# Copies of a finished AFNO chunk: from one DMA queue after the slot's other work to two queues right behind the second layer

## The chip, the core and the metric

The kernel runs on one core of one Trainium2 chip. A core has five instruction streams that run side by side and wait for each other by semaphores: TensorE (PE, matmuls; its weight loads are shown apart as PEld), VectorE (DVE), ScalarE (ACT), GpSimd (POOL) and SyncE (SP, which here only issues DMAs). Sixteen DMA engines carry out what the streams issue. The metric is the device time of one execution in microseconds (us), smaller is better; the figure for a kernel is the median of several runs.

## The reference

The whole layer works on `x` of 4096 rows (a sequence of 4096 points) by 640 features, in float32:

```python
h = _layernorm(x, axis=-1) * (1 + ca) + sa
x = x + ga * _A_ref(h, A_w1, A_b1, A_w2, A_b2)   # AFNO: rfft, a two-layer complex MLP per frequency, soft shrink, irfft
h = _layernorm(x, axis=-1) * (1 + cb) + sb
x = x + gb * _B_ref(h, B_w_gate, B_w_up, B_w_down)   # SwiGLU: (silu(h@wg) * (h@wu)) @ wd, 640 -> 1728 -> 640
```

The six vectors `sa, ca, ga, sb, cb, gb` come from `silu(c) @ w_mod`. The AFNO part takes the Fourier transform along the 4096 points, then for each frequency and each of 4 blocks of 160 features a first complex layer with ReLU and a second complex layer, then a shrink by 0.01, and transforms back.

## The kernel before

The program has three parts in time: a first stage (load, layer norm, first step of the Fourier transform), the AFNO part, and the SwiGLU part, whose order is written out by a planner with costs and due times. The change lies in the AFNO part alone, whose order is written out by hand: each engine runs its instructions in the order in which the Python program issues them, and semaphores are put in for every dependence.

The frequencies are cut into 8 chunks (`ch`), and each chunk into 4 blocks of features (`b`). The loop over `p = 4*ch + b` goes through 29 slots, and the last three slots are written out behind it. One slot works on several (chunk, block) pairs at different depths of the pipeline; `on(f, k)` calls `f(k // 4, k % 4)`:

- `stage_l1(p)`, L679 to L697: first complex layer, on PE, with ReLU and splitting into a high and a low float32 half on ACT and DVE.
- `stage_b` and `evac_b` (L618 to L626) and `evac_rh`, `evac_rl` (L648, L658): second Fourier step of a later chunk and its copies out of PSUM.
- `stage_l2(p - 1)`, L729 and L731: second complex layer on PE. DVE adds the bias and writes the result into the tiles `tt`: two tiles per chunk, `tts[ch, 0]` and `tts[ch, 1]`, each of 128 frequencies by real and imaginary part by 640 features. The pool has two buffers for `tt`, so a chunk's two tiles lie in the buffers that the chunk before it used. Block `b` fills its 160 columns; a tile is complete after `stage_l2` of block 3, which runs in the first slot of the next chunk. In the slot after that, `stage_l2` of the next chunk's block 0 writes into the same buffers.
- `move_x(ch - 1, i)`, L741 to L746, for i = 0 to 3: the copies that this case is about. For each i, two DMAs of 64 partitions by 640 floats bring the real and the imaginary half of 64 frequencies from `tt` into the two halves of a tile `xx` of 128 partitions. i = 0, 1 read `tts[ch, 0]`; i = 2, 3 read `tts[ch, 1]`. `xx` has 5 buffers. In each first slot of a chunk (`b == 0`) from the second chunk on, so 7 times, 8 such DMAs are issued.
- `shrink_parts(p - 5)` on ACT (L751, L752), `shrink(p - 6)` on DVE (L757, or L759 and L760 near the end), `shrink_high(p - 6)` on ACT (L766), `shrink_low(p - 6)` on DVE (L771): the shrink of one `xx` tile and its splitting into `xh` and `xl`. `shrink_low` is the last reader of `xx`.
- `stage_i(p - 7)`, L782 to L786: first inverse Fourier step on PE, copy to `co` on ACT (L785; two buffers), and a store of `co` to the scratch tensor `s2` in device memory, issued by POOL (L786).
- On SP, besides the moves: the slot's loads of `w_mod` rows (tile `wm`, L553; one buffer; DVE sums them up in `acc`, L558 and L560), in every fourth slot the next chunk's input `g` and table `tb` (L313, L299), and near the end parts of `s2` (L843).

On POOL the AFNO slots hold only the `s2` stores (L786) and, around the chunk that carries the edge frequencies (`ch == CE`), some small copies (L629 to L662, L803, L804).

Of the kernel before, what the change touches and what calls it, by code (L numbers as in the profile page):

```python
# [173 lines left out]
def body(tc, x, w1, b1, w2, b2, wg, wu, wd, c, wm, k_fa, k_tb, k_tx, k_bm, k_bx, k_ga, k_ge, k_id, out, dbg=None):  # L174
    nc = tc.nc
    pe, act, dve, pool = nc.tensor, nc.scalar, nc.vector, nc.gpsimd
# [25 lines left out]
    with ExitStack() as top:  # L202
# [35 lines left out]
        with ExitStack() as af:  # L238
# [40 lines left out]
            def weights_high(w, h, l, v, sg, eng=None):  # L279
                if eng:  # L280
                    eng.tensor_scalar(w[:, :, h], v, sg, None, op0=OP.mult)
                else:
                    act.activation(w[:, :, h], v, AF.Copy if isinstance(sg, float) else AF.Identity, scale=sg)

            def weights_low(w, h, l, v, sg):
                dve.scalar_tensor_tensor(w[:, :, l], v, sg, f32(w[:, :, h]), op0=OP.mult, op1=OP.subtract)
# [10 lines left out]
            def load_tb(ch):  # L297
                tb = lp.tile([P, 4, 128], F32, tag="tb", bufs=2, name=f"tb{ch}")
                nc.sync.dma_start(tb, k_tb[:, 4 * ch:4 * ch + 4])  # L299
                tbs[ch] = tb  # L300


            def load_g(ch, us=None):
                if ch not in gs:
                    gs[ch] = fx.tile([P, 4, D], F32, tag="gx", bufs=2, name=f"g{ch}")
                if ch < 2:
                    src = s1[0].rearrange("(u v) (q j e) d -> e u (v q) j d", u=4, e=2, q=4)[ch]
                    for u in us:
                        nc.sync.dma_start(gs[ch][u:P:4], src[u])
                else:  # L310
                    f, e = (1, 2) if ch < 4 else (2, 4)
                    src = s1[f].rearrange("(u v) (q e j) d -> e u (v q) (j d)", u=4, e=e, q=4)[ch % e]
                    nc.sync.dma_start(gs[ch].rearrange("p j d -> p (j d)"), src.rearrange("u r d -> r u d"))  # L313
# [230 lines left out]
            w, h, l, v, _ = prep2[5]  # L544
# [62 lines left out]
            tts = {}  # L607
# [4 lines left out]
            def stage_b(ch, t, tag=None):  # L612
                g, tb = gs[ch], tbs[ch]
                pb = (ps.tile([P, 2, 256], F32, tag=tag, name=f"pb{ch}_{t}") if tag else
                      bank0(1 if t == 4 else 0, [P, 2, 256], f"pb{ch}_{t}"))
                col = slice(128 * t, 128 * t + 128)
                for j in range(4):
                    mm(pb[:, :, 64 * j:64 * j + 64], g[:, j, col], tb[:, j, :], start=True, stop=True)  # L618
                pbs[ch, t] = pb

            def evac_b(ch, t):
                pb = pbs[ch, t]
                z = lp.tile([P, 2, 2, 258], F32R, tag="z", bufs=4, name=f"z{ch}_{t}")
                zs[ch, t] = z
                act.activation(z[:, 0, :, 0:256], pb, AF.Identity, scale=ca1[:, t:t + 1])
                dve.scalar_tensor_tensor(z[:, 1, :, 0:256], pb, ca1[:, t:t + 1],  # L626
                                         f32(z[:, 0, :, 0:256]), op0=OP.mult, op1=OP.subtract)
                if ch == CE:
                    pool.tensor_copy(z[:, 0, :, 0:257:256], f32(edge[:, 0, t]))  # L629
                    pool.tensor_copy(z[:, 1, :, 0:257:256], f32(edge[:, 1, t]))  # L630
                    pool.tensor_copy(z[:, :, :, 257], zero[:, 0, 0])
# [106 lines left out]

            xxs = {}

            def move_x(ch, i):  # L741
                q, h = i // 2, i % 2
                xx = p2.tile([P, D], F32, tag="xx", bufs=5, name=f"xx{ch}_{i}")
                for r in range(2):
                    nc.sync.dma_start(xx[64 * r:64 * r + 64, :], tts[ch, q][64 * h:64 * h + 64, r, :])
                xxs[ch, i] = xx  # L746


# [92 lines left out]
            def load_first_rows(lo, hi, q, e=slice(0, D)):  # L841
                for k in range(2):
                    q.dma_start(cf[k][lo:hi, :, e], s2[lo:hi, 2 * k:2 * k + 2, e])  # L843
# [4 lines left out]
            for p in range(LAST + 1):  # L848
                ch, b = p // 4, p % 4
                on(shrink, p - 6)  # L850
                on(stage_l1, p)


                if p < 4:
                    todo = ([(0, 2)], [(0, 3)], [(1, 4), (1, 0)], [(1, 1)])[p]
                elif b == 0:
                    todo = [(ch, 3)]
                else:
                    todo = [(ch + 1, 4)] * (b == 1) + [(ch + 1, b - 1)]
                todo = [q for q in todo if q[0] < NCH]  # L860
                for q in todo:
                    stage_b(*q)
                    if q[1] < 4:
                        evac_b(*q)
                for f, *a in sums.get(p, ()):
                    f(*a)

                rows = [p + 2] * (p < 4) + [p + 3] * (p > 2)
                for k in rows:
                    on(evac_rh, k)  # L870
                on(tail_l1, p)
                on(shrink_high, p - 6)
                for k in rows:
                    on(evac_rl, k)
                on(tail_low, p)
                on(stage_l2, p - 1)
                if p == 3:
                    stage_b(1, 2)
                    evac_b(1, 2)
                on(stage_i, p - 7)  # L880
                on(shrink_low, p - 6)
                if p < LAST:
                    on(shrink_parts, p - 5)
                if b == 0 and ch:
                    for i in range(4):
                        move_x(ch - 1, i)
                if p == 0:
                    for n in (3, 4):
                        weights_high(*prep2[n])
                    for job in prep2[2:5]:  # L890
                        weights_low(*job)
                if p == 0:
                    pool.dma_start(bm.rearrange("p a b c -> p (a b c)"), k_bm)
                if p == 2 or b == 3 and 2 < ch + 2 < NCH:
                    load_g(ch + 2)
                    load_tb(ch + 2)
                for f, *a in mods.get(p, ()):
                    f(*a)
                if p == LAST - 4:
                    cf += [rp.tile([P, 2, D], F32, tag=tag, name=f"cf{tag}") for tag in ("rm", "rr")]  # L900
                    load_first_rows(rb + 16, rl, nc.sync)
                elif p == LAST - 1:
                    load_first_rows(0, rb - 16, nc.sync)
# [153 lines left out]
        with ExitStack() as ff:  # L1057
# [1081 lines left out]
            for t in range(NS):  # L2139
                for n in range(NW):  # L2140
                    if sum_at(n) == t:
                        a, b = sum_w(n)
# [69 lines left out]
```

## Time and profile before

| what | value |
|---|---|
| median of 3 runs (lowest, highest) | 1471.63 us (1467.69, 1474.02) |
| the profiled execution's own time | 1472.98 us |
| its span, from the first to the last instruction | 1471.2 us |
| mean granted TensorE clock | 0.991 |
| AFNO slots that hold moves | from 94.2 to 277 us of the span |
| PE busy | 1432.1 us (97%) |
| DVE busy | 1054.7 us (72%) |
| ACT busy | 781.7 us (53%) |
| POOL busy | 413.4 us (28%) |

The profile is one execution. A line such as `L731 DVE` is line 731 of the kernel on VectorE; `tt<-pc,b2t` names the tile written and the tiles read. The bracket at the end of a line of the timeline tells how long the engine stood idle before it and what ended that. `SPq` and `POOLq` are DMA issues by SP and POOL. In a view by windows of time, each engine has its busy time and, in brackets, the number of instructions; then come the granted clock, the busy share of the DMA engines and what they moved in GB/s.

### The profile page before, as it was taken

To read this page: it belongs to the slowest core of one execution; us is meant where nothing else is said; L and a number is where in the kernel's file an instruction comes from. 1 tells how busy PE (TensorE), PEld (TensorE's weight loads), DVE (VectorE), ACT (ScalarE), POOL (GpSimd) and SP (SyncE) were. 2 spreads that over 40 slices of the span, in tenths; PEclk is the share of its full clock that TensorE was granted. 3 is DMA by queue.
4 is the path that set the end of the run, shared out by engine and by line. 5 is a ranking of instruction groups with operands and counts; after the bars stand their busy time and mean duration, and the time that the engine had idled before them with its cause. 6 is when DMAs were issued, how large, how long until landed. Compare 5 with 4: busy or idle time off the path is not lost.

```text
span 1471.2 us, 23664 instructions
## 1 busy us (share of the span) xinstructions
PE 1432.1 (97%) x8656; PEld 1353.6 (92%) x8656; DVE 1054.7 (72%) x1901; ACT 781.7 (53%) x1517; POOL 413.4 (28%) x529
## 2 busy tenths in 40 slices
PE   8899999989999999999999999999999999999999
PEld 4699999858878888899999999999999999999998
DVE  8968888877787787657777767787656566466653
ACT  7779989744445455435554545545453344344331
POOL 4500200055544344312433322433411121111111
PEclk9999999989999999999999999999999999999999
DMA  9956566656777986796775995776884345944422
GB/s 361 326 198 205 162 184 210 204 177 224 235 263 241 337 280 206 263 370 197 235 245 191 334 353 181 248 231 215 324 290 137 120 149 195 355 135 144 143 76 83
DMA packets 155927, 332.06 MB, mean 226 GB/s; under 512 B 19873, under 2 KB 79073, under 8 KB 154018
## 3 DMA queue, kind: packets, MB, share of 16 engines
q1 hardware_dynamic: 147426, 313.99, 63.1%
q0 software_dynamic: 6800, 13.93, 2.9%
q10 hardware_dynamic: 1584, 2.62, 0.5%
q8 instruction: 68, 1.11, 0.3%
q14 instruction: 49, 0.40, 0.1%
HBM read 234.35 MB, written 86.64 MB: 218 GB/s over the span
## 4 chain that ended last, share of the span: by engine, by line
PE 69%; issue 9%; DVE 9%; DMA 8%; ACT 3%; POOL 2%; SPq 1%; POOLq 0%; DVEq 0%; ACTq 0%
PE pd L2085 23%; PE pw L1890 8%; PE pw L1892 7%; PE pw L1891 7%; PE pg L1813 3%; PE pg L1814 3%; PE pg L1815 3%; PE pw L1901 2%; PE pw L1903 2%; PE pw L1902 2%; DMA cr<-s 2%; DVE st_a L193 2%; PE py L1533 1%; DMA wt<-td 1%; DVE wb L1347 1%
## 5 line engine op out<-in xcount | busy, mean ns | idle before, releaser
L2085 PE MATMUL pd<-wdh,a 128*128 128x320 f32 x1672 | 381.3, 310 | 1.5 <-DVE x L2057 1.1
L2085 PEld LDWEIGHTS pd<-wdh,a 128*128 128x128 f32 x1672 | 283.0, 188 | 2.5 <-DVE x L2057 1.4
L2085 PE MATMUL pd<-wdl,a 128*128 128x320 f32 x868 | 267.3, 309 | 0.0
L2057 DVE TENSOR_TENSOR x<-x,pd 128x320 f32<-128x320 f32 x384 | 178.2, 481 | 93.9 <-PE pd L2085 90.7
L1347 DVE TENSOR_TENSOR wb<-r,wb 128x512 fp32r<-128x512 f32 (+3 forms) x170 | 167.8, 994 | 16.1 <-ACT wb L1340 15.0
L2085 PEld LDWEIGHTS pd<-wdl,a 128*128 128x128 f32 x868 | 163.1, 188 | 0.5
L1890 PE MATMUL pw<-h,wt 128*128 128x384 f32 x416 | 141.6, 340 | 5.0 <-DMA wt<-td 2.9
L1444 ACT ACTIVATE wdh<-wdr 128x640 fp32r<-128x640 f32 x84 | 60.9, 733 | 149.8 <-PE pd L2085 142.2
L1892 PE MATMUL pw<-h,wt 128*128 128x384 f32 x416 | 140.2, 337 | 0.0
L1891 PE MATMUL pw<-h,wt 128*128 128x384 f32 x416 | 140.0, 337 | 0.0
L1340 ACT ACTIVATE wb<-r 128x768 fp32r<-128x768 f32 (+3 forms) x168 | 115.3, 701 | 20.3 <-PE pg L1815 11.7
L1934 POOL TENSOR_TENSOR sg<-s_x,sg 128x384 f32<-128x384 f32 x24 | 26.4, 1101 | 339.1 <-DVE s_x L1916 304.6
L1890 PE MATMUL pw<-h,wb 128*128 128x384 f32 x312 | 105.0, 337 | 0.0
L1892 PE MATMUL pw<-h,wb 128*128 128x384 f32 x312 | 104.6, 335 | 0.0
L1891 PE MATMUL pw<-h,wb 128*128 128x384 f32 x312 | 104.6, 335 | 0.0
L1937 DVE TENSOR_TENSOR a<-sg,a 128x384 fp32r<-128x384 f32 x104 | 80.2, 775 | 32.9 <-ACT a L1936 32.6
L1813 PE MATMUL pg<-ht,wb 128*128 128x512 f32 x260 | 103.7, 399 | 0.0
L1814 PE MATMUL pg<-ht,wb 128*128 128x512 f32 x260 | 102.0, 392 | 0.0
L1815 PE MATMUL pg<-ht,wb 128*128 128x512 f32 x260 | 101.6, 391 | 0.0
L1448 DVE TENSOR_TENSOR wdl<-wdr,wdh 128x640 fp32r<-128x640 f32 x84 | 74.6, 898 | 27.2 <-ACT wdh L1444 27.1
L1890 PEld LDWEIGHTS pw<-h,wt 128*128 128x128 f32 x416 | 78.6, 189 | 7.8 <-DMA wt<-td 3.5
L1516 POOL TENSOR_TENSOR cr<-cr,gab 128x640 f32<-128x640 f32 x28 | 48.2, 1720 | 119.3 <-DMA cr<-s 116.4
(278 smaller groups left out, 3380.7 us busy)
## 6 DMA issues: line engine op xcount, KB each, us to landing
wt<-td SPq DMA_DIRECT2D x104, 512.0 KB, 5.2
hs<-ho SPq DMA_DIRECT2D x52, 512.0 KB, 5.1
h<-hs SPq DMA_DIRECT2D x32, 768.0 KB, 9.9
r<-in_B_w_up_dram SPq DMA_DIRECT2D x36, 640.0 KB, 5.7
r<-in_B_w_gate_dram SPq DMA_DIRECT2D x36, 640.0 KB, 5.1
wdr<-wdd SPq DMA_DIRECT2D x35, 640.0 KB, 4.1
td<-wt SPq DMA_DIRECT2D x25, 512.0 KB, 4.7
xx<-tt SPq DMA_DIRECT2D x56, 160.0 KB, 3.8
```

Source lines behind the costliest of these rows:

```text
L1340: def high(ks, e=slice(0, c), copy=lambda o, i: act.activation(o, i, AF.Copy)):
L1347: dve.tensor_tensor(wbs[t, n][:, 1, ks, e], raw[t, n][:, ks, e], f32(wbs[t, n][:, 0, ks, e]), op=OP.subtract)
L1448: dve.tensor_tensor(l[:, f], wdraw[t, p][:, f], f32(h[:, f]), op=OP.subtract)
L1813: mm(b, wh, hh, start=(kk == 0), stop=False)
L1814: mm(b, wh, hl, start=False, stop=False)
L1815: mm(b, wl, hh, start=False, stop=(kk == 4))
L1890: mm(b, w(0, kp), a[:, kp, 0], start=start and kp == 0, stop=False, skip_group_check=not start)
L1891: mm(b, w(0, kp), a[:, kp, 1], start=False, stop=False, skip_group_check=not start)
L1892: mm(b, w(1, kp), a[:, kp, 0], start=False, stop=kp == 1, skip_group_check=not start)
L1937: Step("V", cv_ + 0.1, lambda: dve.tensor_tensor(o[:, 1], sg, f32(o[:, 0]), op=OP.subtract), (("ah", key),), ("act", t, fc, a), free=("sg" ...
L2057: dve.tensor_tensor(x2[:, e], x2[:, e], x[0][:, :320], op=OP.add)
L2085: mm(pd[g, hf][0][:, :320], l, m, start=i == 0, stop=i == len(s) - 1 and not (last and len(gs) > 1))
```

## The change

`move_x` gets a parameter for the engine that issues its DMAs. Its calls are put forward within the slot: they stand right behind `stage_l2(p - 1)` now, ahead of `stage_i(p - 7)`, `shrink_low(p - 6)` and `shrink_parts(p - 5)`. The copies for i = 0 and 1 stay on SP, and those for i = 2 and 3 are issued by POOL.

```diff
-            def move_x(ch, i):
+            def move_x(ch, i, eng=nc.sync):
                 q, h = i // 2, i % 2
                 xx = p2.tile([P, D], F32, tag="xx", bufs=5, name=f"xx{ch}_{i}")
                 for r in range(2):
-                    nc.sync.dma_start(xx[64 * r:64 * r + 64, :], tts[ch, q][64 * h:64 * h + 64, r, :])
+                    eng.dma_start(xx[64 * r:64 * r + 64, :], tts[ch, q][64 * h:64 * h + 64, r, :])
                 xxs[ch, i] = xx
...
                 on(stage_l2, p - 1)
+                if b == 0 and ch:
+                    for i in range(4):
+                        move_x(ch - 1, i, pool if i > 1 else nc.sync)
                 if p == 3:
...
                 if p < LAST:
                     on(shrink_parts, p - 5)
-                if b == 0 and ch:
-                    for i in range(4):
-                        move_x(ch - 1, i)
                 if p == 0:
```

In the order that results, the instructions of PE, ACT and DVE are the same and in the same order as before. On SP, 28 of the 56 moves are gone and nothing else changes place. On POOL, four moves stand in each of the seven slots ahead of that slot's store of `co`; in the slot p = 12 they stand behind the two small edge copies L803 and L804. From the second of the seven slots on, the tile `xx` of i = 3 lies in the buffer that `shrink_low(p - 6)` of the same slot still reads, so its copies wait for that instruction of DVE, before the change and after it.

## The prediction

> **What bounds the kernel now.** The page's first table says which engine is full over the whole span.
>
> ```profile
> PE 1432.1 (97%) x8656; PEld 1353.6 (92%) x8656; DVE 1054.7 (72%) x1901; ACT 781.7 (53%) x1517; POOL 413.4 (28%) x529
> ```
>
> PE is, but the change touches only the AFNO slots, some 200 us of 1471, so I read these by themselves: the windows view in stretches of about one chunk, with one row for all that follows.
>
> ```profile
> 100.00:128.00 28.00, 26.99 (x207) 26.38 (x206) 24.35 (x48) 25.31 (x53) 1.13 (x2) 1.00 0.54 167
> 128.00:158.00 30.00, 28.76 (x226) 28.50 (x226) 25.19 (x51) 26.90 (x56) 3.50 (x12) 1.00 0.58 182
> 158.00:188.00 30.00, 29.66 (x227) 28.97 (x226) 25.59 (x50) 28.02 (x59) 6.74 (x27) 1.00 0.58 176
> 188.00:220.00 32.00, 30.04 (x240) 29.45 (x239) 26.30 (x52) 27.95 (x57) 2.17 (x4) 1.00 0.56 174
> 220.00:248.00 28.00, 28.00 (x221) 28.00 (x220) 24.42 (x48) 27.12 (x56) 2.17 (x4) 1.00 0.54 175
> 248.00:279.00 31.00, 29.53 (x223) 28.82 (x222) 26.25 (x52) 25.22 (x54) 2.71 (x5) 1.00 0.67 210
> 300.00:1471.20 1171.20, 1152.24 (x6765) 1103.17 (x6763) 801.79 (x1363) 536.89 (x1023) 355.83 (x412) 0.99 0.67 225
> ```
>
> After the length come PE, PEld, DVE, ACT and POOL. PE stands still for only 1.01, 1.24, 0.34, 1.96, 0.00 and 1.47 us in the six chunks, and ACT and DVE are close behind it. So whatever the change frees elsewhere, **a chunk can hardly shrink by more than its idle time on PE**. The last row says that behind 300 us PE is busy 1152 of 1171 us: what AFNO saves shifts that part forward as a block, and I count it in full.
>
> Next, the view of waits, from 80 to 300 us, for DVE, ACT and PE.
>
> ```profile
> DVE tt L731 <- DMA xx<-tt: 12.0, 6, 2.7
> ACT r L704 <- DVE u L697: 7.9, 8, 1.9
> PE pi L782 <- DVE u L697: 1.9, 2, 1.2
> PE pl L679 <- DVE tt L737: 1.8, 1, 1.8
> PE pc L729 <- DVE tt L731: 0.4, 1, 0.4
> ```
>
> The first row is DVE's largest wait: the add that fills `tt` for a new chunk waits until the moves have read the old chunk out of that buffer. The timeline shows this, first slot and second slot of a chunk (the first two lines are the first boundary, then the second one with SP and POOL, then the waits of the other five).
>
> ```profile
> 93.69 0.89 DVE L731 TENSOR_TENSOR tt<-pc,b2t 128x320 f32<-128x320 f32 x2
> ...
> 100.14 0.49 DVE L731 TENSOR_TENSOR tt<-pc,b2t 128x320 f32<-128x320 f32 x1
> 103.36 0.49 DVE L731 TENSOR_TENSOR tt<-pc,b2t 128x320 f32<-128x320 f32 x1 [2.73 <-DMA xx<-tt]
> ...
> 121.29 0.89 DVE L731 TENSOR_TENSOR tt<-pc,b2t 128x320 f32<-128x320 f32 x2
> 121.81 6.26 SPq L745 DMA_DIRECT2D xx<-tt  x8
> 121.93 0.54 POOL L786 DMA_DIRECT2D s<-co  x1 [6.41 <-ACT co L785]
> 122.09 0.81 DVE L771 TENSOR_TENSOR xl<-xx,xh 128x640 fp32r<-128x640 f32 x1
> 128.11 0.49 DVE L731 TENSOR_TENSOR tt<-pc,b2t 128x320 f32<-128x320 f32 x1
> 128.16 5.12 SPq L553 DMA_DIRECT2D wm<-in_w_mod_dram  x2
> 130.66 0.49 DVE L731 TENSOR_TENSOR tt<-pc,b2t 128x320 f32<-128x320 f32 x1 [2.06 <-DMA xx<-tt]
> 160.87 0.49 DVE L731 TENSOR_TENSOR tt<-pc,b2t 128x320 f32<-128x320 f32 x1 [1.88 <-DMA xx<-tt]
> 190.52 0.49 DVE L731 TENSOR_TENSOR tt<-pc,b2t 128x320 f32<-128x320 f32 x1 [2.35 <-DMA xx<-tt]
> 222.21 0.49 DVE L731 TENSOR_TENSOR tt<-pc,b2t 128x320 f32<-128x320 f32 x1 [1.64 <-PE pl L679]
> 250.75 0.49 DVE L731 TENSOR_TENSOR tt<-pc,b2t 128x320 f32<-128x320 f32 x1 [1.74 <-DMA xx<-tt]
> 280.67 0.49 DVE L731 TENSOR_TENSOR tt<-pc,b2t 128x320 f32<-128x320 f32 x1 [1.23 <-DMA xx<-tt]
> ```
>
> SP starts the moves as soon as the first `tt` is full (121.81, against 121.29 + 0.49), so no instruction ahead of them in the program holds them back. They take SP 6.26 us for eight, and the last lands too late. The first add of the next chunk (128.11) does not wait; the second, which needs the moves of i = 2 and 3, waits 2.06 us. At the fifth boundary the view names PE, but I take the 1.64 us for the same wait, since it stands at the same place of a chunk. Seven waits: 13.6 us.
>
> **The change part by part.** *The place.* Putting the calls forward in the slot moves them past instructions of PE, DVE and ACT, which SP and POOL do not run. On SP nothing is passed. On POOL the moves now stand ahead of the slot's `s2` store. Alone the place is worth 0, by the 121.81 above; what it buys is that POOL does not wait for `co` first.
>
> *The split.* What one issue costs on either stream comes from the views of lines 745, 786 and 318 (the last are small copies of the first stage, on POOL and SP).
>
> ```profile
> L745 SPq DMA_DIRECT2D xx<-tt x56: 469/590/1893, 94.2 to 276.3; - x56
> DMA to landing us min/median/max: 2.6/3.8/5.7
> ...
> L786 POOL DMA_DIRECT2D s<-co x28: 542/542/591, 114.9 to 298.8; - x28
> DMA to landing us min/median/max: 2.4/3.9/6.3
> ...
> L318 POOL DMA_DIRECT2D g<-xa x4: 572/597/797, 45.2 to 49.8; - x4
> DMA to landing us min/median/max: 2.5/3.7/4.8
> ```
>
> POOL has never issued these moves, so its price lies between the nearest rows: 0.54 us (L786) and 0.80 us (the longest of L318). I take 0.6, the median of L318, whose copies go from SBUF to SBUF as the moves do. Four issues put the last one's start 3 x 0.6 = 1.8 us behind the end of the pair of adds, and it lands 3.9 us later: 5.7 us. With the ends of the rows it is 3 x 0.54 + 2.4 = 4.0 to 3 x 0.8 + 6.3 = 8.7 us. At the first boundary the pair ends at 94.58 and the second add could start at 100.14 + 0.49 = 100.63, 6.05 us later; at the second it is 128.60 - 122.18 = 6.42 us. The wait of i = 3 for `shrink_low` (122.09 + 0.81 = 122.90) ends before POOL has issued its first two moves. So at median prices the wait is gone with 0.3 us to spare, and at the far end 2.6 us of it remain. SP's own four start as they do now and land 1.8 + 3.8 = 5.6 us behind 121.81, at 127.4, ahead of 128.11.
>
> *What that is worth.* A shorter wait of DVE counts where another engine stood still for it. On PE these are the three rows above: 1.9 + 1.8 + 0.4 = 4.1 us, at the first, second and fourth boundary. At the third, fifth and sixth PE shows no gap, so I take 0.5 us for all three (bounds 0 and their DVE waits, 5.3). At the last, near the end of AFNO, DVE waits 1.23 us and PE shows nothing; I take 0.3 (bounds 0 and 1.23). Against that I set 0.9 us for what is left of waits because the bursts run close: **4.1 + 0.5 + 0.3 - 0.9 = 4.0 us saved**.
>
> *The store behind the moves.* POOL's `s2` store of that slot, now at 121.93, comes some 2.7 us later. `co` has two buffers and one store per slot of about 7 us, so its buffer is wanted two slots on, some 14 us later: nothing is paid. If that cover went, ACT's copy L785 would wait up to 2.7 us. The small edge copies on POOL in slots 12 to 16 stand ahead of the moves or a slot behind them, with POOL busy 6.74 of 30 us at most: nothing.
>
> *SP's loads.* `wm` (128.16) is issued about 2.5 us earlier. Nothing waits for it to speak of, but it enters the DMA engines while POOL's moves are under way, and the `s2` store leaves that place. How full these engines are during a burst:
>
> ```profile
> 123.00:131.00 8.00, 8.00 (x66) 8.00 (x65) 5.55 (x11) 7.88 (x19) 0.54 (x1) 1.00 0.90 232
> 244.00:251.00 7.00, 7.00 (x57) 7.00 (x57) 4.87 (x11) 6.72 (x15) 0.54 (x1) 1.00 0.97 264
> ```
>
> The last two columns are their busy share and GB/s: 0.90 and 0.97 busy. [...]
>
> **The rivals.** *B, the DMA engines are the limit.* Eight moves are 1280 KiB, 1.31 MB, which at 232 to 264 GB/s takes 5.0 to 5.7 us; the first lands 2.6 us after 121.81, the last 7/8 of that later, at 128.8 to 129.4, and with a `wm` load (0.33 MB, 1.2 to 1.4 us) between them at 130.0 to 130.8. Then the second add waits 1.4 to 2.2 us, as now, or the first add takes over part of it. Saved: 0 to 1 us, time 1471. For it speaks the share of 0.90 to 0.97. Against it: at 0.97 they moved more than at 0.90, so a high share is not yet the limit, and SP's 6.26 us for eight issues would give the same pace.
>
> *C, PE's record hides slack.* A busy PE may be waiting for its operands. ACT runs without a break in most of these slots, and its waits for DVE's `u` are 7.9 us; if all of that fell and PE kept up, 7.9 us would be saved: 1463.7. Against it: PE busy 28.00 of 28.00 in the fifth chunk.
>
> *D, slower: POOL issues late.* If one move costs POOL k us, the last lands 3k + 3.9 us behind the pair; today the second add starts 130.66 - 122.18 = 8.5 us behind it. So **POOL decides against the change from k = 1.5 us on**. At k = 2.2 the wait is 2.1 us longer at each of 7 boundaries, 14.7 us; of today's 13.6 us a third reached PE, but little slack would be left, so I take 9: 1480.6. Against it: no POOL issue of DMAs in the rows above took over 0.8 us. [...]
>
> That the change does nothing at all belongs to B.
>
> **How the numbers follow.** The sum is made against the profiled execution, whose 1472.98 us are 1471.2 of span and 1.8 around it: 1472.98 - 4.0 = 1469.0. The median of the runs is 1.35 lower, so the forecast is 1471.63 - 4.0 = 1467.6. Chances: forecast 0.49 (1465.5 to 1469.5), B 0.25 (1470 to 1472), C 0.11 (1462 to 1465), D 0.15 (1474 to 1486). The range takes in the forecast, B, most of C and the near part of D, and the spread of the runs: 1461 to 1477. About 0.5% (7.4 us) is what a measurement of this kernel can tell from no change; below 1464.3 lies half of C and a few stray cases, above 1479.0 the larger part of D: faster 0.10, same 0.78, slower 0.12.
>
> **What would show it.** In the changed kernel's waits, `DVE tt L731 <- DMA xx<-tt` should fall from 12.0 to under 4 us, POOL's issues of L745 should take 0.5 to 0.8 us each, and PE's waits for `u` L697 and `tt` L737 after a boundary should be gone, with the AFNO part some 4 us shorter. B shows as waits of 1.4 us and more at L731, maybe on the first add, with moves that land over 5 us after their issue. C shows as chunks of under 27 us. D shows as POOL issues of 1.5 us and more. I am wrong in the sum if the waits go and the chunks keep their length: then ACT or PE was the bound and the 4.1 us were not DVE's to give.

## The result: slower, and the wait has moved to the first add

| | before | after |
|---|---|---|
| median of 6 runs (lowest, highest) | 1472.83 us (1467.69, 1474.34) | 1479.80 us (1478.55, 1482.60) |
| ratio, 95% interval | | 1.0056 [1.0037, 1.0076] |
| profiled execution: time, span | 1472.98, 1471.2 us | 1481.95, 1480.2 us |

The change costs 7 us by the medians, and 5.4 to 11.2 us by the interval. The forecast was 1467.6 us with a range of 1461 to 1477; the result lies above the range.

The engines do the same work as before (the page's first table, after):

```profile
PE 1432.5 (97%) x8656; PEld 1354.0 (91%) x8656; DVE 1054.2 (71%) x1901; ACT 780.4 (53%) x1517; POOL 426.5 (29%) x557
```

Only POOL is busier, by 13 us: 28 issues at half a microsecond. So the time went into waiting. The view of waits of the changed kernel, 80 to 310 us (us in all, times, longest):

```profile
DVE tt L731 <- DMA xx<-tt: 19.7, 6, 4.9
DVE tt L731 <- PE pb L618: 3.6, 1, 3.6
PE pi L782 <- DVE u L697: 4.6, 5, 2.1
PE pc L729 <- DVE tt L731: 4.5, 4, 2.5
PE pl L679 <- DVE tt L737: 3.3, 1, 3.3
```

The wait that was to fall from 12.0 to under 4 us is 19.7 us, with a seventh of 3.6 at the same place that the view puts down to PE: 23.3 us where there were 13.6. It reaches PE now: the three PE rows are 12.4 us against 4.1 before, and this difference of 8.3 us is about the size of the result. The timeline of the same kernel shows where the wait sits: the pair of adds ahead of the first boundary, then all seven boundaries, with SP and POOL around the second.

```profile
95.94 0.89 DVE L731 TENSOR_TENSOR tt<-pc,b2t 128x320 f32<-128x320 f32 x2
104.94 0.89 DVE L731 TENSOR_TENSOR tt<-pc,b2t 128x320 f32<-128x320 f32 x2 [2.59 <-DMA xx<-tt]
...
122.96 0.89 DVE L731 TENSOR_TENSOR tt<-pc,b2t 128x320 f32<-128x320 f32 x2
123.48 3.97 SPq L745 DMA_DIRECT2D xx<-tt  x4
124.15 2.07 POOL L745 DMA_DIRECT2D xx<-tt  x4 [6.97 <-DVE tt L731]
126.20 0.58 POOL L786 DMA_DIRECT2D s<-co  x1
127.55 9.89 SPq L553 DMA_DIRECT2D wm<-in_w_mod_dram  x2
134.66 0.89 DVE L731 TENSOR_TENSOR tt<-pc,b2t 128x320 f32<-128x320 f32 x2 [4.93 <-DMA xx<-tt]
165.54 0.89 DVE L731 TENSOR_TENSOR tt<-pc,b2t 128x320 f32<-128x320 f32 x2 [2.91 <-DMA xx<-tt]
196.63 0.89 DVE L731 TENSOR_TENSOR tt<-pc,b2t 128x320 f32<-128x320 f32 x2 [3.94 <-DMA xx<-tt]
231.10 0.89 DVE L731 TENSOR_TENSOR tt<-pc,b2t 128x320 f32<-128x320 f32 x2 [2.95 <-DMA xx<-tt]
261.35 0.89 DVE L731 TENSOR_TENSOR tt<-pc,b2t 128x320 f32<-128x320 f32 x2 [3.64 <-PE pb L618]
294.35 0.89 DVE L731 TENSOR_TENSOR tt<-pc,b2t 128x320 f32<-128x320 f32 x2 [2.33 <-DMA xx<-tt]
```

Before, a boundary had two rows of `x1`: the first add ran on time and the second waited. Now it has one row of `x2`: **the first add waits, and the second follows at once**. The first add overwrites the tile whose four copies are SP's. POOL does what was expected: its four issues take 2.07 us and begin 0.3 us behind the pair. What the copies take from issue to landing is another matter. First the view of line 745 (ns minimum, median, maximum of an issue; then us to landing), then the DMA view of the same kernel from 120 to 132 us (copies, KB, median us to landing):

```profile
L745 SPq DMA_DIRECT2D xx<-tt x28: 469/588/2743, 96.5 to 285.4; - x28
L745 POOL DMA_DIRECT2D xx<-tt x28: 516/523/575, 97.1 to 285.8; - x28
...
DMA to landing us min/median/max: 2.4/5.1/8.8
```

```profile
xx<-tt SPq DMA_DIRECT2D x4, 160.0 KB, 7.8
xx<-tt POOLq DMA_DIRECT2D x4, 160.0 KB, 4.2
```

A move lands 5.1 us after its issue where it took 3.8, and at the second boundary SP's moves take 7.8 (by the two of the four whose landing is recorded). SP is held up in issuing too (3.97 us for four, 2.74 for one).

The chain can be followed by position. Ahead of the first move the profiled execution is already 2.25 us late (95.94 against 93.69); no copy of the change has run by then, so this is not the change's. The second add of the last boundary comes at 294.35 + 0.40 = 294.75 against 280.67: 14.1 us late. So the seven boundaries cost 11.8 us in this execution. Behind them some of it is given back; the span ends 9.0 us later.

### The profile page after: what moved, and what is told of

Its sections match the earlier page's. It is cut to its first block, busy times and chain, and to the rows that moved or that the text cites. A ratio compares the mean times of both kernels' runs of the same rounds, so it can differ in the third digit from the quotient of the medians.

```text
span 1480.2 us, 23684 instructions
## 1 busy us (share of the span) xinstructions
PE 1432.5 (97%) x8656; PEld 1354.0 (91%) x8656; DVE 1054.2 (71%) x1901; ACT 780.4 (53%) x1517; POOL 426.5 (29%) x557
## 4 chain that ended last, share of the span: by engine, by line
PE 72%; DMA 12%; DVE 9%; ACT 3%; issue 2%; POOL 1%; SPq 1%; DVEq 0%; POOLq 0%; ACTq 0%
PE pd L2085 24%; PE pw L1890 8%; PE pw L1892 8%; PE pw L1891 7%; PE pg L1814 3%; PE pg L1813 3%; PE pg L1815 3%; DMA xx<-tt 3%; PE pc L729 2%; PE pw L1901 2%; PE pw L1902 2%; PE pw L1903 2%; PE pl L679 2%; DMA wt<-td 2%; PE py L1533 1%
## 5 line engine op out<-in xcount | busy, mean ns | idle before, releaser
L1347 DVE TENSOR_TENSOR wb<-r,wb 128x512 fp32r<-128x512 f32 (+3 forms) x170 | 167.9, 995 | 13.7 <-ACT wb L1340 12.4
```

The costliest lines, as they stand in the source:

```text
L1347: dve.tensor_tensor(wbs[t, n][:, 1, ks, e], raw[t, n][:, ks, e], f32(wbs[t, n][:, 0, ks, e]), op=OP.subtract)
```

## The experiments

One measure serves for most of them: how long after the first issue of a burst (i) the first tile, which the first add overwrites, and (ii) both tiles have been read out. It is the latest recorded landing of the copies concerned, the median of a run's seven bursts, worked out from the landings in the trace. Up to half of SP's landings are not recorded (28 of 56 before, 13 of 28 after), so a figure can be too low. The first adds of the changed kernel give a reading that does not need them: they start 8.5 to 11.2 us behind the first issue of their burst, median 10.3. The ratio is to the kernel before, measured with the run.

| kernel | first tile | both | ratio, 95% interval |
|---|---|---|---|
| before | 6.1 | 9.0 | 1 |
| after | 10.0 | 10.0 | 1.0056 [1.0037, 1.0076] |
| e4, all on POOL | 6.1 | 8.6 | 1.0005 [0.9987, 1.0022] |
| e3, divided by half of xx | 5.0 | 8.3 | 1.0002 [0.9979, 1.0026] |
| e8, after, POOL on the other half | 8.6 | 8.6 | 1.0012 [0.9998, 1.0027] |
| e13, the same with all computation | 8.6 | 8.8 | 1.0021 [1.0005, 1.0037] |
| e2, first tile first, opposite halves | 5.3 | 8.1 | 0.9971 [0.9954, 0.9988] |
| e9, first tile first, same half | 5.0 | 9.8 | 1.0050 [1.0033, 1.0066] |
| e10, e2 with the store on SP | 5.4 | 7.7 | 0.9958 [0.9942, 0.9973] |

Four theories went in. **H**: SP and POOL run in step over the same 64 partitions and slow each other's packets. **S**: the DMA engines share their time between the queues, so SP's four copies end where eight used to end. **G**: copies issued by GpSimd are slow by themselves. **A**: the first tile has to have the first copies of both queues.

**e1, the place alone.** All eight on SP, behind `stage_l2`.

```diff
-                        move_x(ch - 1, i, pool if i > 1 else nc.sync)
+                        move_x(ch - 1, i)
```

> The moves stand behind the second layer as in the changed kernel, but all eight are issued by SP. All three theories (H: two queues in step meet on the same 64 partitions and their packets take twice the time; S: the DMA engines share out packets between queues, and SP's half comes last behind POOL's moves and store; G: copies issued by GpSimd are slow by themselves) expect the time of the kernel before, a ratio of 0.998 to 1.002, and waits of 12 to 14 us at L731, since the place should be worth nothing. A ratio of 1.004 and more would put the loss on the place.

Measured: 1471.23 against 1471.23 us, ratio 1.0005 [0.9984, 1.0025]. The place is worth nothing that this run can tell (the interval leaves up to 3.7 us), so the loss is the split's.

**e4, all on POOL.**

```diff
-                        move_x(ch - 1, i, pool if i > 1 else nc.sync)
+                        move_x(ch - 1, i, pool)
```

> All eight moves are issued by POOL, none by SP. G expects the worst of all: waits of over 4 us at each boundary and a ratio over 1.008. H expects that one queue meets itself no more than before, so landings 3 to 5 us after the issue and a ratio of 0.997 to 1.003, with POOL's 0.52 us per issue against SP's 0.63. S expects the same, as nothing is shared but with the loads of wm.

Measured: 1.0005 [0.9987, 1.0022], with waits as before. A burst that POOL issues alone is read out as fast as SP's (8.6 us against 9.0): G falls.

**e2, each tile shared between the queues, halves opposite.** SP copies i = 0 and 2 (partitions 0 to 63), POOL i = 1 and 3 (64 to 127), and POOL takes the halves of `xx` in the other order.

```diff
-                for r in range(2):
+                for r in ((0, 1), (1, 0))[h]:
...
-                        move_x(ch - 1, i, pool if i > 1 else nc.sync)
+                        move_x(ch - 1, i, pool if i % 2 else nc.sync)
```

> SP copies the lower 64 frequencies of both tiles (i = 0, 2), POOL the upper 64 (i = 1, 3) and in the opposite order of real and imaginary, so that the two queues never read the same 64 partitions, and in step never write the same. Bytes, queues and number of issues are those of the changed kernel. H expects the waits at L731 to fall under 8 us in total, over 300 GB/s in the bursts, and a ratio to before of 0.995 to 1.000. S and G expect the changed kernel's result: waits of about 20 us and a ratio of 1.004 to 1.007.

Measured: 0.9971 [0.9954, 0.9988], faster than both kernels. The waits of e2:

```profile
DVE tt L731 <- DMA xx<-tt: 4.2, 3, 1.8
DVE tt L731 <- PE pb L618: 2.4, 1, 2.4
DVE tt L731 <- PE pl L692: 1.4, 1, 1.4
DVE tt L731 <- PE pl L679: 0.8, 1, 0.8
```

Together 8.8 us at L731, all on the second add. So two queues can help; but e2 changes the division and the halves at once, so H and A both fit.

**e3, divided by the half of `xx`.** SP issues r = 0 of every piece, POOL r = 1: both read the same source partitions and write opposite ones.

```diff
-                    eng.dma_start(xx[64 * r:64 * r + 64, :], tts[ch, q][64 * h:64 * h + 64, r, :])
+                    (pool if r else nc.sync).dma_start(xx[64 * r:64 * r + 64, :], tts[ch, q][64 * h:64 * h + 64, r, :])
```

> SP copies the real half of every piece, POOL the imaginary half: the two queues never write the same 64 partitions, but in step they read the same. H, if the writing side is what meets, expects the result of the split by halves (waits under 8 us, ratio 0.995 to 1.000); if the reading side is, the changed kernel's (about 20 us, 1.004 to 1.007). S and G expect the changed kernel's result in either case.

Measured: 1.0002 [0.9979, 1.0026], waits 12.6 us on the second add. Between the two, which told nothing apart by itself.

**e5 and e6, two attempts to part H from A, both inconclusive.** e5 has the changed kernel's division, with SP beginning on the upper half (i = 1 before 0).

```diff
-                for r in range(2):
+                for r in ((0, 1), (1, 0))[q]:
...
-                    for i in range(4):
+                    for i in (1, 0, 2, 3):
```

> The division of the changed kernel is kept (SP the first tile, POOL the second), but SP starts with the upper 64 frequencies (i = 1, then 0) and POOL, which starts with the lower 64 (i = 2, then 3), goes through real and imaginary in the opposite order: in step the two queues read and write different halves of the partitions. H (queues that meet on the same 64 partitions take twice the time) expects most of what the split by halves gained: waits at L731 of under 12 us, ratio to before 0.996 to 1.002. The rival A says that the split by halves won because each tile was shared between the queues, so that the first add no longer hung on SP's late half alone; it expects the changed kernel's result here: waits of about 20 us on the first add, ratio 1.003 to 1.007.

Measured: 1.0055 [1.0038, 1.0072]. But `xx` of i = 0, which ACT needs first, comes last on SP, and a new wait appears beside the old one:

```profile
DVE tt L731 <- DMA xx<-tt: 15.9, 7, 3.5
ACT cl L751 <- DMA xx<-tt: 13.1, 6, 3.4
```

e6 gives both queues pieces of both tiles (SP i = 0, 3; POOL i = 2, 1), in the same order of halves. `make_x`, not shown, only makes the tile `xx` that `move_x` then fills.

```diff
-                        move_x(ch - 1, i, pool if i > 1 else nc.sync)
+                        make_x(ch - 1, i)
+                    for i in (0, 3, 2, 1):
+                        move_x(ch - 1, i, pool if i in (1, 2) else nc.sync)
```

> Each tile is shared between the queues (SP i = 0, then 3; POOL i = 2, then 1), as in the split by halves, but both queues go through lower and upper half and through real and imaginary in the same order, so in step they meet on the same 64 partitions. H expects the changed kernel's slow bursts: under 240 GB/s, waits at L731 of 15 us and more, ratio 1.003 to 1.008. A expects the result of the split by halves: waits of about 9 us, ratio 0.995 to 0.999.

Measured: 1.0083 [1.0059, 1.0108], waits 22.8 us on the first add. The first tile's second half comes last on POOL here, so that H and A expect the same after all.

**e8 and e9, one thing at a time.** e8 is the changed kernel with only the partitions of POOL's copies exchanged; e9 is e2 with only POOL's copies put on SP's half.

```diff
 e8, to the changed kernel
-                    eng.dma_start(xx[64 * r:64 * r + 64, :], tts[ch, q][64 * h:64 * h + 64, r, :])
+                    s, d = (1 - h, 1 - r) if q else (h, r)
+                    eng.dma_start(xx[64 * d:64 * d + 64, :], tts[ch, q][64 * s:64 * s + 64, r, :])
 e9, to e2
-                for r in ((0, 1), (1, 0))[h]:
+                for r in range(2):
-                    eng.dma_start(xx[64 * r:64 * r + 64, :], tts[ch, q][64 * h:64 * h + 64, r, :])
+                    eng.dma_start(xx[64 * r:64 * r + 64, :], tts[ch, q][0:64, r, :])
```

> The changed kernel with its own division (SP the four copies of the first tile, POOL those of the second), its own order, place and queues; but each of POOL's copies reads the other 64 partitions and writes the other 64 partitions of xx than in the changed kernel, so that SP and POOL never read or write the same half at the same time. What it leaves out: the second tile's halves come out exchanged, so its frequencies and its real and imaginary parts are mixed up; the amount of work is the same. H (two queues in step on the same 64 partitions slow each other's packets): bursts of 280 GB/s and more, waits at L731 under 12 us in the AFNO part, ratio at most 1.002. S (a queue's share of the engines decides) and A (the first tile must have the first copies of both queues): the waits stay on the first add at about 20 us, ratio 1.004 to 1.007.

> The division of e2 (both queues begin with the first tile, SP its first two copies, POOL its other two), but POOL's copies read the same lower 64 partitions as SP's, and in the same order of the two halves of xx. What it leaves out: the upper 64 frequencies of each tile are not copied, the lower ones stand in their place; the number and size of the copies is the same. H: packets of 200 ns and bursts of about 200 GB/s again, waits at L731 of 15 us or more in the AFNO part, ratio 1.003 or more. A: only the division counts, so the result of e2 comes again, waits of about 9 us and a ratio of 0.995 to 0.999.

Measured: e8 1.0012 [0.9998, 1.0027], e9 1.0050 [1.0033, 1.0066]. The waits of e8, then of e9:

```profile
DVE tt L731 <- DMA xx<-tt: 12.5, 6, 3.0
DVE tt L731 <- PE pl L692: 1.9, 1, 1.9
```

```profile
DVE tt L731 <- DMA xx<-tt: 22.0, 7, 4.6
```

With after and e2 these make a square. Putting the queues on opposite halves takes 1.4 us off the burst in the changed division (10.0 to 8.6) and 1.7 in e2's (9.8 to 8.1), and 0.4 to 0.8% off the time. Dividing the other way makes the burst only 0.2 to 0.5 us shorter, but lets the first tile go at 5.0 to 5.3 us. With the halves in step that gains next to nothing (1.0056 and 1.0050): the wait only goes back to the second add, as e9's timeline shows.

```profile
127.84 0.49 DVE L731 TENSOR_TENSOR tt<-pc,b2t 128x320 f32<-128x320 f32 x1
...
132.20 0.49 DVE L731 TENSOR_TENSOR tt<-pc,b2t 128x320 f32<-128x320 f32 x1 [3.87 <-DMA xx<-tt]
```

With the halves opposite it gains another 0.4%. So the halves count, as H says, and A holds where they do not collide. e8's waits came out above the "under 12 us" that H set (14.4), and its bursts reach 280 GB/s only towards their end (at the second boundary, first issue at 119.28 us, the DMA view shows 171 to 265 GB/s from 120.0 to 122.7 us and 401 to 461 from 127.2 to 128.1); why they are slower at first was not tried.

**e13, e8 with all of the computation kept.** POOL copies i = 3 before i = 2, and the halves of `xx` in the other order.

```diff
-                for r in range(2):
+                for r in ((0, 1), (1, 0))[q]:
...
-                    for i in range(4):
+                    for i in (0, 1, 3, 2):
```

> The changed kernel with POOL's four copies in the opposite order (i = 3 before i = 2, and the two halves of xx exchanged in order), so that SP and POOL start on opposite halves; all of the computation is kept. The half: as e8, ratio 0.9995 to 1.003, first-add waits of about 2 to 3 us. S or A: as the changed kernel, 1.004 to 1.007.

Measured: 1.0021 [1.0005, 1.0037], waits of 13.8 + 2.1 us, 2.0 to 3.7 at a time on the first add. That confirms e8.

**m1 and m2, the copies by themselves.** In m1 each burst was to wait for VectorE's refill of the source, but the refill was cut into rows, so bursts ran into each other. Two of its seven bursts (`cp(i, s, d)` gives a copy from partitions s to d; L is 0, U is 64; `sp` and `q` issue on SP and POOL):

```python
fill()
for i in range(4):
    sp.dma_start(*cp(i, L, L))
    q.dma_start(*cp(i + 4, L, L))
fill()
for i in range(4):
    sp.dma_start(*cp(i, L, L))
    q.dma_start(*cp(i + 4, U, U))
```

> The disputed cost by itself: nothing of the reference is computed, the output is filled with copied rows. Seven bursts of eight copies of 64 partitions x 2560 bytes from SBUF to SBUF, three times over, each burst behind VectorE's refill of the source, with no other work on the chip: SP alone on the lower half; SP alone with halves as before; POOL alone on the lower half; then SP and POOL four each, SP always lower to lower and POOL lower to lower, upper to upper, lower to upper, upper to lower. H (two queues on the same 64 partitions): lower/lower about 200 GB/s, packets twice as long, the eight land about 6.5 us after the first issue; upper to upper 280 GB/s and more, landed in about 4.5 us. If reading is what collides, lower to upper is as slow as lower to lower and upper to lower as fast as upper to upper; if writing, the other way round; if either is enough, both are slow. If SP alone on the lower half is as slow as both queues on it, it is the half and not the second queue. S or A alone: all four mixed bursts take the same time.

Measured: over three repetitions the last landing of a mixed burst came behind that of the burst ahead by 5.6 to 6.2 us lower/lower, 4.6 to 4.9 upper to upper, 5.5 to 7.0 lower to upper and 5.5 to 6.6 upper to lower, and SP alone on the lower half took 0.8 us per copy. That left open whether it is the second queue or the half.

m2 gives each of the eight copies its own part of the source and refills all of it in one instruction, so that bursts stand apart:

```diff
-            fill()
+            dve.tensor_copy(tt, src)
```

> The copies by themselves again, with one refill of the whole source ahead of each burst, so that a burst starts when the one before has landed; nothing of the reference is computed. Ten bursts of eight copies, three times: SP alone lower to lower; POOL alone lower to lower; SP alone over both halves in turn; SP four lower to lower with POOL's four lower to lower, upper to upper, lower to upper, upper to lower; and the orders of the changed kernel, of e8 and of e2. If the half is what is slow, whoever copies: SP alone on the lower half about 0.8 us per copy (205 GB/s) against 0.64 over both, the mixed burst lower/lower about 6 us from the first to the last landing against 4.5 for upper to upper, and the changed kernel's order about 1.5 us behind e8's. If the second queue is what is slow: SP alone lower to lower 0.64 per copy. Reading or writing: whichever of lower to upper and upper to lower is as slow as lower to lower names the side, and if both are, it is either.

The last of the eight landed so long behind the first issue (us, three repetitions, from the landings in the trace):

| burst | last landing |
|---|---|
| SP alone, lower half | 8.0, 7.9, 7.9 |
| POOL alone, lower half | 8.2, 8.2, 8.0 |
| SP alone, both halves in turn | 7.1, 7.4, 7.0 |
| SP lower, POOL lower | 8.1, 8.0, 8.0 |
| SP lower, POOL upper | 7.4, 7.4, 7.4 |
| SP lower, POOL reads lower, writes upper | 8.0, 8.1, 8.0 |
| SP lower, POOL reads upper, writes lower | 7.9, 7.9, 8.0 |
| order of the changed kernel | 7.8, 7.8, 7.8 |
| order of e8 | 7.4, 7.3, 7.2 |
| order of e2 | 7.4, 7.4, 7.3 |

The refills of the source show the same roughly, since each waits for the burst ahead of it (the bracket holds the burst and 0.1 to 0.5 us more). The timeline of m2, second repetition; ahead of these rows ran lower with lower, lower with upper, the order of the changed kernel, and that of e8.

```profile
163.34 2.83 DVE L208 COPY tt<-src 128x5120 f32<-128x5120 f32 x1 [8.44 <-DMA xx<-tt]
173.71 2.83 DVE L212 COPY tt<-src 128x5120 f32<-128x5120 f32 x1 [7.54 <-DMA xx<-tt]
...
206.91 2.83 DVE L224 COPY tt<-src 128x5120 f32<-128x5120 f32 x1 [8.18 <-DMA xx<-tt]
217.13 2.83 DVE L228 COPY tt<-src 128x5120 f32<-128x5120 f32 x1 [7.39 <-DMA xx<-tt]
```

This corrects H: **it is the half, not the second queue**. SP alone on the lower half is as slow (7.9 to 8.0 us) as the two queues on it (8.0 to 8.1). Its copies land 0.80 us apart (160 KB each, 205 GB/s); over both halves they land 0.68 to 0.72 apart. Meeting on one side is enough here, reading or writing (8.0 to 8.1 and 7.9 to 8.0 us); but in these bursts that side stays on its half for all eight copies. In e3 the queues read the same half in step and change it with every copy, and its burst took 8.3 us, close to e2's 8.1.

SP's halves in turn, as in the kernel before, already avoid the collision (7.9 to 8.0 us with SP on the lower half alone), so in m2 a second queue has nothing to win: 7.2 to 7.4 us against 7.0 to 7.4. In the whole kernel it has something to win: both tiles are read out at 8.1 us in e2 and 7.7 in e10, and at 9.0 before. There SP alone issues the last of its eight copies 4.4 to 5.7 us behind the first, while in e2 the two streams have issued all eight after 1.9 to 2.6 us; that this makes the difference was not tried by itself.

The third finding: in the changed kernel's order SP's four copies land 2.4, 4.1, 7.0 and 7.8 us after the first issue, against 2.3, 3.2, 3.9 and 4.7 for the first four of SP alone. That fits S, without the kernel around it. The queues do not get equal shares either. The DMA view of the changed kernel from 125 to 131 us (packets, MB, share of the engines; q0 is POOL's queue, with its store, q1 is SP's, with `wm`):

```profile
q0 software_dynamic: 209, 0.77, 59.5%
q1 hardware_dynamic: 219, 0.45, 37.1%
```

POOL's queue moved 1.7 times as much. Four copies are 256 packets of 2560 bytes on SP's queue in m2 and 128 packets of 5120 bytes on POOL's (beside 64 of 4 bytes on each), and in the first burst of the changed kernel POOL's queue shows the same 128 and 64; whether the larger packets are why POOL's queue moved more was not tried by itself.

What m2 doesn't give is the full size: by itself the collision costs 0.5 us per burst (7.8 to 7.3), in the kernel 1.4. There the bursts meet the store and `wm`; that these make the rest was not tried by itself.

**e10, the store out of POOL's queue.** e2, with the `s2` store of the slot that moves issued by SP behind the moves.

```diff
-                pool.dma_start(s2[4 * J:4 * J + 4].rearrange("k n d -> (k n) d"), co)
+                (nc.sync if (4 * ch + i + 7) % 4 == 0 and 4 * ch + i + 7 < NP else pool).dma_start(
+                    s2[4 * J:4 * J + 4].rearrange("k n d -> (k n) d"), co)
```

> e2 with the s2 store of the slot that moves (L786) issued by SP behind its moves and ahead of wm, so that POOL's queue holds the four moves alone. S: the store and POOL's larger packets take the engines from SP's last moves; with the store gone from POOL's queue the waits at L731 fall from e2's 8.8 us to 3 to 5, ratio 0.994 to 0.997. H alone: the store made no difference, e2's result again, 0.9971 within its interval, unless SP waits for co before wm, which then comes 2 to 3 us later.

Measured: 1465.99 against 1471.05 us, 0.9958 [0.9942, 0.9973], the lowest ratio so far; both tiles are read out at 7.7 us instead of 8.1. Its waits on DVE:

```profile
DVE tt L731 <- DMA xx<-tt: 2.8, 3, 1.3
DVE acc L560 <- DMA wm<-in_w_mod_dram: 1.7, 3, 1.1
DVE acc L558 <- DMA wm<-in_w_mod_dram: 1.5, 2, 1.4
DVE tt L731 <- PE pl L679: 1.4, 2, 0.7
DVE tt L731 <- PE pi L784: 0.4, 1, 0.4
```

4.6 us at L731 where e2 had 8.8. The two intervals of e2 and e10 overlap, so the time alone does not part them; the waits fell by half.

**e7, e11 and e12, the price of the waits.** A third buffer for `tt` takes the waits away without a second queue. e7 gives it to the pool that holds `tt`.

```diff
-                    h = hp.tile([P, 2, 258], F32R, tag="h", bufs=8, name=f"h{ch}_{b}_{o}")
+                    h = hp.tile([P, 2, 258], F32R, tag="h", bufs=7, name=f"h{ch}_{b}_{o}")
-                        tts[ch, q] = p2.tile([P, 2, D], F32, tag="tt", bufs=2, name=f"tt{ch}_{q}")
+                        tts[ch, q] = p2.tile([P, 2, D], F32, tag="tt", bufs=3, name=f"tt{ch}_{q}")
```

> The kernel before, moves at their old place and all on SP, with three buffers for the tile tt instead of two (and seven instead of eight for the tile h, to make room). The next chunk's first add then finds a free buffer, and its second hangs on the first four moves alone, which have landed by then. This prices the wait without any change in the DMAs' queues. My forecast's reasoning (4.1 us on PE hang on 13.6 us of waits) expects waits at L731 of under 2 us and a ratio of 0.995 to 0.998. If PE or ACT were the bound, the waits go and the ratio stays at 0.999 to 1.001.

Measured: 1.0105 [1.0084, 1.0127], the slowest of all. The waits at L731 are gone, but a wait at the start of AFNO, which the kernel before does not have, hides the answer; that it comes from the larger pool, which shifts what lies behind it, is argued and not shown (waits of e7, 40 to 310 us):

```profile
DVE w2a L286 <- POOL w2a L281: 18.7, 1, 18.7
```

e11 puts the third buffer in the pool of `h`, so that nothing else moves.

```diff
-                    h = hp.tile([P, 2, 258], F32R, tag="h", bufs=8, name=f"h{ch}_{b}_{o}")
+                    h = hp.tile([P, 2, 258], F32R, tag="h", bufs=5, name=f"h{ch}_{b}_{o}")
-                        tts[ch, q] = p2.tile([P, 2, D], F32, tag="tt", bufs=2, name=f"tt{ch}_{q}")
+                        k = (2 * ch + q) % 3
+                        tts[ch, q] = (hp if k == 2 else p2).tile([P, 2, D], F32, tag=f"tt{k}", bufs=1, name=f"tt{ch}_{q}")
```

> The kernel before, all eight moves on SP in their old place, with a third buffer for tt (in the pool of h, which gives up three of its eight buffers), so that the first add of a new chunk writes a tile whose copies ended a chunk ago and only the second add can wait. It gives the price of the waits without a second queue. If they cost what the prediction put on them (4.1 to 5 us, of 13.6 us on VectorE): ratio 0.9965 to 0.998, waits at L731 under 2 us. If wm, which the adds no longer hold back, or ACT is late next: waits at L560 or L704 grow and the ratio is 0.999 to 1.001.

Measured: 1467.18 against 1471.05 us, 0.9971 [0.9954, 0.9987]. No wait at L731 (L732 in this kernel) is left; the loads of `wm` come next:

```profile
DVE acc L558 <- DMA wm<-in_w_mod_dram: 4.9, 2, 2.9
DVE acc L560 <- DMA wm<-in_w_mod_dram: 4.8, 4, 1.8
```

So by e11's time the waits are worth 4.3 us (1.9 to 6.8). The profiled executions give a second reading, which leaves out what lies ahead of the seven boundaries and behind them: from the first add of the pair ahead of the first boundary to the second add of the last one it is 187.0 us before, 183.1 in e11 and 183.0 in e7 as well, so 3.9 us less in both; 184.1 in e2, 181.6 in e10 and 198.8 in the changed kernel. PE stands still in this stretch for 6.0 us before, 3.7 in e11 and 13.4 in the changed kernel.

e12 is e10 with this buffer (the same four lines, changed in e10).

> e10 (two queues on opposite halves, the store on SP) with the third tt buffer of e11. If the waits at L731 were all that was to be had, no more than e10 or e11 alone: 0.995 to 0.997. If both add up: 0.993. If wm is late next: L560 and L558 wait 5 us and more and the ratio is that of e11.

Measured: 0.9957 [0.9935, 0.9979], no better than e10. The waits at L731 (L732 here) are gone and those for `wm` are 5.5 and 1.8 us. The gains don't add up: there is one wait to take away, and `wm` is late next.

## Why the prediction was wrong, step by step

- *A chunk can't shrink by more than PE's idle time, and the waits are worth about 4 us.* Right: e11 takes them away and gains 4.3 us by its time, 3.9 at the boundaries of its profile. That e2 gains 4.3 as well is in part luck: 8.8 us of its waits are left, and its boundaries give 2.9.
- *The place alone is worth 0.* Right (e1).
- *POOL's issues cost 0.6 us, between 0.54 and 0.80.* Right up to a little: 0.516 to 0.575, median 0.523 us. Rival D, whose time came nearest the result, was wrong in its premise, and close by luck: POOL was never late in issuing. No run shows a k near its 1.5 or 2.2: a move's issue took POOL 0.575 us at most in the changed kernel and 0.825 in e4 and e10. (Its sum has a slip, too: at k = 2.2 the wait is 2.0 us longer, 14 us at seven boundaries, not 14.7.)
- **The step that failed:** "SP's own four start as they do now and land 1.8 + 3.8 = 5.6 us behind 121.81, at 127.4, ahead of 128.11." They start as before, but the last lands 10.0 us after the first issue (11.0 at the second boundary). The 3.8 us was the landing time of SP's queue with only POOL's store beside it, and the prediction used it for two queues of moves at once. In the same way POOL's last was to land "5.7 us" behind the pair at median prices; it landed 7.3 to 9.0 us behind it, median 7.9, which is at the far end of the prediction's 4.0 to 8.7. Its store behind it, from the same queue, is under way then (the stores issued from 120 to 132 us land after 7.1 us, median), and a burst with that store on SP is shorter (7.7 us in e10, 8.1 in e2). The runs put two things in the place of this step: beside a second queue SP's fourth copy ends with the last of the burst (7.8 us instead of 4.7 in m2), and a burst whose queues keep to the same half takes longer (10.0 us in the changed kernel, 8.6 in e8).
- The 0.9 us set "for what is left of waits because the bursts run close" is the term that should have carried this. It measured as 23.3 us of waits instead of 13.6: a gain of 4 us turned into a loss of 7.
- *Rival B* had the place of the new wait ("maybe on the first add") and landings of over 5 us, but priced it at 0 to 1 us saved. It missed what two queues do to the order: the first tile, which lay wholly on SP, was then ready only when the last copy of all was (both at 10.0 us). Before, SP's order had let it go at 6.1 of 9.0 us, just ahead of the first add. And it took 232 to 264 GB/s from bursts whose halves come in turn; on one half at a time m2 has 205.
- *`wm` earlier, "nothing waits for it to speak of".* Right in the changed kernel (one wait of 1.4 us at L560), though it is what is late next in e11.
- The store behind the moves was set at nothing for `co`. That holds, but by e10 it costs the moves some 0.4 us of a burst (8.1 to 7.7).

## What to carry to other kernels

For these copies a second queue did not raise the pace (7.2 to 7.4 us a burst in m2, against 7.0 to 7.4 for SP alone); it changed the order in which they ended. Ask which buffer is wanted first, and give its copies the front of every queue, for a whole buffer on one of two queues was ready here only when both were nearly done (10.0 us in the changed kernel, 5.3 in e2). And let copies of 64 partitions alternate halves on the reading and the writing side, across queues as well as within one: in m2 that is 7.0 to 7.4 us a burst against 7.9 to 8.2 on the lower half alone.

## What else the runs showed of the hardware

TensorE's granted clock was not the same in the two executions: the changed kernel has four windows at 0.87 and 0.96 between 190 and 280 us, where the kernel before has 1.00. By the author's reading that is part of what the waits cost. The windows of the changed kernel (the columns are length, PE, PEld, DVE, ACT, POOL, clock, DMA share, GB/s):

```profile
130.00:140.00 10.00, 6.54 (x49) 6.08 (x48) 5.27 (x11) 5.83 (x12) 0.55 (x1) 1.00 0.59 172
...
190.00:200.00 10.00, 6.70 (x51) 6.44 (x51) 5.50 (x12) 6.32 (x15) 0.54 (x1) 0.96 0.66 177
200.00:210.00 10.00, 10.00 (x73) 9.94 (x73) 7.29 (x16) 7.39 (x16) 0.54 (x1) 0.87 0.33 97
...
260.00:270.00 10.00, 7.24 (x45) 6.79 (x44) 7.15 (x15) 6.30 (x14) 0.54 (x1) 0.87 0.79 278
270.00:280.00 10.00, 10.00 (x80) 10.00 (x79) 9.55 (x19) 9.49 (x21) 0.54 (x1) 0.96 0.40 139
```

In the windows at 190 and 260 us PE stands still for 3.3 and 2.8 us, and clock worth 1.7 us is lost around each (0.04 and 0.13 of 10 us). Together with the 8.3 us of PE's waits this is about the 11.8 us that the boundaries cost. The kernel before, e2 and e10 show 1.00 in every window from 90 to 290 us. But not every stop is followed by a lower clock: in the window at 130 us PE stands still for 3.5 us, and the clock is 1.00 there and in the next window. The kernel before pays later, at the end of AFNO:

```profile
290.00:300.00 10.00, 7.40 (x39) 6.01 (x40) 8.87 (x16) 3.47 (x9) 1.63 (x3) 0.96 0.71 286
300.00:310.00 10.00, 10.00 (x27) 5.84 (x26) 5.03 (x8) 2.68 (x5) 3.04 (x2) 0.69 0.62 191
```

From 290 to 310 us the changed kernel shows 1.00, and by position on VectorE it gets back 2.7 us of its 14.1 in the same stretch, between 300 and 316 us of the kernel before. That the clock is the cause of this was only read from the two traces, not tried.
